# Storing a one-row decode result from two pairs of neighbouring partitions, on two queues

## The chip, the core and the metric

The kernel runs on one core of one Trainium2 chip. Its inputs lie in the chip's memory (HBM), and its result goes back there. The metric is the device time of one execution in microseconds (us). The kernel before takes 99.54 us (median of three runs, 99.52 to 99.94).

A core has five engines with instruction streams of their own: TensorE (PE, matrix products), VectorE (DVE), ScalarE (ACT), GpSimd (POOL) and SyncE (SP), which here only waits and starts transfers. They signal each other with semaphores. Transfers between HBM and the on-chip memory (SBUF, 128 partitions) are carried out by DMA engines, which SP and ACT feed through a queue each. PE writes its products to PSUM, an accumulator memory that also has 128 partitions.

## The reference

One token, a vector `x` of 1024 numbers, passes through attention over a window of 4096 cached positions and, in parallel, through a small MLP:

```python
xn = layernorm(x)
# A: 32 query heads on 4 key/value heads, the last W = 4096 positions
q = xn @ wq                                     # 1024 -> 32 x 128
p = softmax((q . k) * 128**-0.5)                # per head, over 4096 positions
A = (p . v) @ wo                                # 4096 -> 1024
# B: second layernorm, then an MLP of 3584 hidden units
B = gelu(layernorm(xn) @ w1 + b1) @ w2 + b2     # 1024 -> 3584 -> 1024
return x + A + B                                # 1 x 1 x 1024, bfloat16
```

Everything is bfloat16 in memory. The weights and the cached keys and values come to 39.86 MB, and all of it has to be read once; the result is 2 KB.

## The kernel before, in words

**Loads.** SP issues the large loads in the order w1, k, wq, then (once buffers come free) w2, v and, last, wo. Each has a semaphore of its own, or one for each chunk. wo is loaded in four chunks of 20, 8, 3 and 1 rows (`WO_CHUNKS`), where a "row" means the 1024 output columns that belong to one of 32 contraction steps of 128. ACT issues three small loads at the start, on lines 204 to 206: b1 (16 pieces of 448 bytes), x and b2 (one piece of 2048 bytes each).

**Vector times matrix.** In all products with a weight matrix the vector is the stationary operand (it is loaded into PE as weights, LDWEIGHTS) and the matrix streams through (MATMUL). PE's array is used as four column tiles of 32 columns. For w2 and wo the 1024 output columns are cut into four quarters, and quarter `a` is made in column tile `a`, so it lands in PSUM on the partitions 32a to 32a+31 of one bank (`quad`). All 28 steps of w2 and all 32 steps of wo accumulate onto the same four quarters, and before them `x` and `b2` are added there with a product with a one (line 488). One step is a call of `row`: four weight loads and four matmuls with 256 streamed columns, one for each quarter.

A weight tile has 32 columns, but only one of them is wanted. `put` is given 32 neighbouring columns of `VEC`, beginning with the wanted one, so the wanted result stands on the first partition of each quarter: 0, 32, 64 and 96. The other 31 partitions collect sums that nobody reads. `VEC` holds the MLP's hidden vector (`GT`, 28 columns), 32 zero columns, the attention's output (`OT`, 32 columns) and 32 more zero columns.

**Loops on PE.** The steps of w2 and wo are rolled into loops (`rolled`, line 160): 7 trips of 4 steps each, where one trip has 16 weight loads and 16 matmuls. The addresses are in registers. At the start of a trip every operand's address is worked out with one register addition from that of the first operand of its kind (lines 177 to 179): 15 additions for the 16 matrix operands and 3 for the 4 vector operands. Several such additions are put into one instruction, FUSED_REGOPS. After the matmuls come a further FUSED_REGOPS (line 182) and the branch back (line 184).

**The end.** The trips of the wo loop wait for a count (`s_go`) that SP raises when a chunk has landed (lines 560 to 562): the first chunk releases five trips, the second chunk two. The last four steps are written out behind the loop: steps 28 to 30 wait for the third chunk, step 31 for the fourth. The weights of step 31 are loaded early, by four matmuls with a single column (`oneb`) into a bank that nobody reads, so that only its four matmuls are left when the last chunk arrives. Then ACT copies the PSUM bank to `ORow` in SBUF (128 partitions, 256 columns each), ACT starts the store of the four wanted rows, 512 bytes each, and SP waits for it:

```python
act.wait_ge(PE.sem, C["fin"])
C["a_out"] = ACT.mark(act.activation(out=ORow[:, :], in_=PS[:, 7 * 512:7 * 512 + 256], func=ACTF.Copy))
act.wait_ge(ACT.sem, C["a_out"])
act.dma_start(out_rows, ORow[0:128:32, :]).then_inc(s_out, 16)
sp.wait_ge(s_out, 16)
```

SP has nothing to do between its last release of the wo loop and this wait.

Of the kernel before, what the change touches and what calls it, by code (L numbers as in the profile page):

```python
# [10 lines left out]
D = 1024  # L11
# [7 lines left out]
FC = F // 128  # L19
# [4 lines left out]
LOOPED = 28  # L24
STEP = 4
# [3 lines left out]
NB = 64  # L29
OUTSIDE = -1e30  # L30
PAD = 32


class Track:
# [16 lines left out]
def bass_parallel_sum__sliding_block_cached__mixer_channel_mlp__decode_kernel(  # L51
# [18 lines left out]
    pe, dve, act, pool, sp = nc.tensor, nc.vector, nc.scalar, nc.gpsimd, nc.sync  # L70

    def sems(name, n):
        return [nc.alloc_semaphore(f"{name}{i}") for i in range(n)]

    s_xrow, s_b1, s_b2, s_w1, s_w2, s_out, s_go, s_row = (
        nc.alloc_semaphore(n) for n in ("s_xrow", "s_b1", "s_b2", "s_w1", "s_w2", "s_out", "s_go", "s_row"))
# [7 lines left out]
    ACT = Track(nc, "S_ACT")  # L84
    POOL = Track(nc, "S_POOL")

    def sb(name, shape, d):
        return nc.alloc_sbuf_tensor(name, shape, d)

    f32, bf16 = dt.float32, dt.bfloat16  # L90
    identb = sb("identb", [128, 128], bf16)
# [10 lines left out]
    oneb = sb("oneb", [128, 32], bf16)  # L102
    XBR = sb("XBR", [1, 2 * D], bf16)
    XT16 = sb("XT16", [128, 16], f32)
    msx = sb("msx", [128, 8], f32)
    XNTb = sb("XNTb", [128, KC + PAD], bf16)
    YT16 = sb("YT16", [128, 16], f32)
    msy = sb("msy", [128, 8], f32)
    EXPW = sb("EXPW", [128, 1], f32)
    YTb = sb("YTb", [128, KC + PAD], bf16)  # L110
    Hs = sb("Hs", [128, 1024], bf16)
    Qs = sb("Qs", [128, 1024], bf16)
    ORow = sb("ORow", [128, 256], bf16)
# [1 line left out]
    LB = sb("LB", [128, 8 * 144], bf16)  # L115
    HT = sb("HT", [128, FC], f32)
    U2 = sb("U2", [128, FC], f32)
    VEC = sb("VEC", [128, FC + PAD + 32 + PAD], bf16)
    GT = VEC[:, 0:FC]
    OT = VEC[:, FC + PAD:FC + PAD + 32]  # L120
    MXP = sb("MXP", [128, 3], f32)
    MXH = sb("MXH", [1, HQ], f32)
    MXQ = sb("MXQ", [1, 4 * HQ], f32)
# [14 lines left out]
    W2 = W1[:, 0:FC * D]  # L138
    WA = WW[:, KC * F:KC * F + KC * NQ]
    PS = nc.alloc_psum_tensor("PS", [128, 8 * 512], f32)  # L140
# [9 lines left out]
    out_rows = out.rearrange("b s (a n) -> (b s a) n", a=4)  # L150

    C = {}
# [60 lines left out]
    def fill(out, pattern, base, step, op=ALU.not_equal, value=1.0):  # L213
        pool.wait_ge(POOL.sem, POOL.cnt)
        return POOL.mark(pool.affine_select(
            out=out, in_=out, pattern=pattern, compare_op=op, fill=value, base=base, channel_multiplier=step))

    C["oneb"] = POOL.mark(pool.memset(oneb[:, :], 1.0))
    C["onesf"] = POOL.mark(pool.memset(onesf[:, :], INV_D))
    POOL.mark(pool.memset(XNTb[:, KC:KC + PAD], 0.0))  # L220
    C["pads"] = POOL.mark(pool.memset(YTb[:, KC:KC + PAD], 0.0))

# [18 lines left out]
    C["mask"] = fill(OUTM[:, :].rearrange("k (s g) -> k s g", g=2), [[0, 256], [1, 2]], 0, -1, value=0.0)  # L241
    C["vec"] = POOL.mark(pool.memset(VEC[:, :], 0.0))
    POOL.mark(pool.memset(BLI[:, :], 1.0))
# [44 lines left out]
    for r in range(KC):  # L288
        last = pe.matmul(xt[:, r:r + 1], lhsT=XBR[0:1, r:D:KC], rhs=oneb[0:1, 0:1])  # L289
# [40 lines left out]
    def lowered(ap, weights):  # L330
        return pe.lower_ap(ap, for_matmul_weights=weights) if isinstance(ap, bass.AP) else ap

    def tile(out, lhsT, rhs, size, at, load=True, start=False):
        return pe.add_instruction(mybir.InstMatmult(  # L334
            name=nc.get_next_instruction_name(), engine=pe.engine,
            ins=[lowered(rhs, False), lowered(lhsT, True)], outs=[pe.lower_ap(out)],
            start_tensor_calc=start, stop_tensor_calc=True, bass_skip_group_check=True, ldweights=load,
            tile_size=size, tile_position=at))

    def put(out, lhsT, rhs, a, load=True, start=False):  # L340
        return tile(out, lhsT, rhs, (128, 32), (0, 32 * a), load, start)

    def full(out, lhsT, rhs, load, start=False):
        return tile(out, lhsT, rhs, (128, 128), (0, 0), load, start)

    def part(t, bank):
        at = (bank + t // 4) * 512
        return PS[32 * (t % 4):32 * (t % 4) + 32, at:at + 512]
# [3 lines left out]
    for t in range(7):  # L352
        last = tile(part(t, 0), oneb[64:65, :], b1v[:, :, :, 4 * t:4 * t + 4], (32, 32), (64, 32 * (t % 4)), t < 4, True)
# [36 lines left out]
    for i in range(8):  # L390
        n = 128 if i < 4 else 96
        last = pe.matmul(PSb[:, 2 * 1024 + 128 * i: 2 * 1024 + 128 * i + n], lhsT=Hs[0:n, 512 * (i // 4) + i % 4:512 * (i // 4 + 1):4],
                         rhs=identb[0:n, 0:n], is_transpose=True)
# [18 lines left out]
    dve.wait_ge(POOL.sem, C["consts"])  # L412
    C["d_GT"] = DVE.mark(dve.tensor_tensor(out=GT, in0=HT[:, :], in1=U2[:, :], op=ALU.mult))

# [15 lines left out]
    for i in range(8):  # L430
        last = pe.matmul(PSb[:, 7 * 1024 + 128 * i: 7 * 1024 + 128 * (i + 1)], lhsT=Qs[:, i * 128:(i + 1) * 128],
                         rhs=identb[:, :], is_transpose=True)
# [7 lines left out]
    for e in range(4):  # L440
        last = pe.matmul(PS[:, 6 * 512 + 32 * e:6 * 512 + 32 * e + 32], lhsT=REP4[:, e * 128:(e + 1) * 128], rhs=QT[:, :])
    C["rep"] = PE.mark(last)
    LB8 = LB[:, :].rearrange("p (e x) -> p e x", x=144)
    for eng, track, qs in ((dve, DVE, (0, 1)), (act, ACT, (2, 3))):
        eng.wait_ge(PE.sem, C["rep"])
        eng.wait_ge(POOL.sem, C["lb"])
        for q in qs:
            dst = LB8[32 * q:32 * q + 32, :, 32 * q:32 * q + 16]
            src = PS[32 * q:32 * q + 32, 6 * 512:6 * 512 + 128].rearrange("p (e h) -> p e h", e=8)
# [2 lines left out]

    quad = [PS[32 * a:32 * a + 32, 7 * 512:7 * 512 + 256] for a in range(4)]

    def row(vec, ws, load=True):
        for a in range(4):
            last = put(quad[a], vec, ws[a], a, load)
        return last

    def steps(label, data, c0, n, sem=None, ready=None):  # L460
        def rows(ws, vs):
            for r in range(STEP):
                row(vs[r], ws[4 * r:4 * r + 4])

        rolled(label, n // STEP, (
            (lambda o: [data[:, bass.ds(o + j * 256, 256)] for j in range(4 * STEP)], STEP * D, False),
            (lambda o: [VEC[:, bass.ds(o + c0 + r, 32)] for r in range(STEP)], STEP, True)), rows, sem, ready)

    pe.wait_ge(DVE.sem, C["lb", 1])
    pe.wait_ge(ACT.sem, C["lb", 3])  # L470
    for half in range(2):
        for i in range(NPAIR):
            for e in range(4):
                for n in range(2 * half, 2 * half + 2):
                    at = (i * 4 + n) * 2048 + e * 512
                    last = full(PS[:, n * 512:(n + 1) * 512], LB[:, e * 288 + i * 128:e * 288 + i * 128 + 128],
                                KD[:, at:at + 512], n % 2 == 0)
# [7 lines left out]
    for a in range(4):  # L485
        for i in range(2):
            src = XBR[0:1, i * D + a * 256:i * D + (a + 1) * 256]
            tile(quad[a], identb[0:1, 0:32], src, (32, 32), (0, 32 * a), i == 0, i == 0)

    for half in range(2):  # L490
        pe.wait_ge(DVE.sem, C["mx", half])
# [20 lines left out]
            in_=Pb[:, n * 512:(n + 1) * 512].rearrange("p (c i h) -> p c i h", i=NPAIR, h=16)))  # L512
    C["tot"] = DVE.mark(dve.tensor_reduce(out=SUMP[:, :], in_=SUMS[:, :], axis=AX.X, op=ALU.add))
    pe.wait_ge(s_w2, 16)
    steps("w2", W2, 0, FC)
    pe.wait_ge(DVE.sem, C["tot"])
    C["rows"] = PE.mark(pe.matmul(PS[:, 5 * 512:5 * 512 + 1], lhsT=SAME[:, :], rhs=SUMP[:, :]))
    pe.wait_ge(DVE.sem, C["zo"])
# [30 lines left out]
    for dq in range(4):  # L549
        last = pe.matmul(PS[:, 6 * 512 + 160:6 * 512 + 192], lhsT=E4[:, dq * 128:(dq + 1) * 128],  # L550
                         rhs=OD[:, dq * 32:(dq + 1) * 32], start=(dq == 0), stop=(dq == 3))
    C["o2"] = PE.mark(last)
    for _ in range(3):
        turn_over()
    dve.wait_ge(PE.sem, C["o2"])
    dve.wait_ge(DVE.sem, DVE.cnt)
    C["OT"] = DVE.mark(dve.tensor_scalar(
        out=OT, in0=PS[:, 6 * 512 + 160:6 * 512 + 192], scalar1=REC[:, 0:1], scalar2=None, op0=ALU.mult))
    went = 0
    for j, n in enumerate(WO_CHUNKS[:-2]):  # L560
        went += n
        sp.wait_ge(s_wo[j], 16)
        sp.nop(hint="wo").then_inc(s_go, went // STEP - (went - n) // STEP)
    steps("wo", WA, FC + PAD, LOOPED, s_go, C["OT"])
    pe.wait_ge(s_wo[-2], 16)
    for c in range(LOOPED, 32):
        vec = VEC[:, FC + PAD + c:FC + PAD + c + 32]
        if c == 31:
            for a in range(4):
                put(PS[32 * a:32 * a + 32, 3 * 512:3 * 512 + 1], vec, oneb[:, 0:1], a, True, True)  # L570
            pe.wait_ge(s_wo[-1], 16)
        last = row(vec, [WA[:, c * D + a * 256:c * D + (a + 1) * 256] for a in range(4)], c < 31)
    C["fin"] = PE.mark(last)

    pe.br_lt(zero, 0, on_true="L_main", on_false="L_end").branch_hint(ending)
# [1 line left out]

    act.wait_ge(PE.sem, C["fin"])
    C["a_out"] = ACT.mark(act.activation(out=ORow[:, :], in_=PS[:, 7 * 512:7 * 512 + 256], func=ACTF.Copy))  # L579
    act.wait_ge(ACT.sem, C["a_out"])  # L580
    act.dma_start(out_rows, ORow[0:128:32, :]).then_inc(s_out, 16)
    sp.wait_ge(s_out, 16)

    return nc

# [27 lines left out]
```

## Time and profile before

| what | value |
|---|---|
| median of three runs | 99.54 us (99.52 to 99.94) |
| the profiled execution's own time | 99.53 us |
| its span, first to last instruction | 98.3 us (98.28) |
| time outside the span | 1.25 us |
| read from HBM | 39.86 MB, 406 GB/s over the span |
| PE busy / DVE busy / ACT busy | 49.0 / 31.5 / 9.6 us |
| mean granted TensorE clock | 0.844 of full |
| ACT's issue of the result's store (line 581) | 603 ns, from 96.58 us on |

The profile gives times in us from the start of the span. "PE" is matmuls and "PEld" weight loads; a "q" behind an engine's name (ACTq, SPq, PEldq) means its sequencer, that is waits, branches, register arithmetic and the issuing of transfers, which do not count as busy time. The bracket at the end of a row gives the engine's idle time before it and what ended it; "issue" is idle time for which the profile shows no wait. The trace also has each transfer's packets and the moments at which a transfer's semaphore counts up. A semaphore of a transfer rises by 16 in all.

### The profile page before, as it was taken

How to read it: one execution, taken by the hardware profiler on the slowest of the kernel's cores; microseconds unless marked ns; L12 is line 12 of the kernel's file. 1: busy time of each engine (PE TensorE's matmuls, PEld its weight loads, DVE VectorE, ACT ScalarE, POOL GpSimd, SP SyncE). 2: the span in 40 equal slices, each digit the busy share in tenths (PEclk: the TensorE clock that was granted, in tenths of full speed). 3: DMA queues.
4: the chain of work that ended last, by engine and by line, in shares of the span. 5: the costliest groups of instructions: out<-in, count | busy, mean ns of one | idle time of the engine just before them, and what ended most of it. 6: DMA issues, size and time to landing. Idle time of an engine off the chain costs nothing.

```text
span 98.3 us, 1233 instructions
## 1 busy us (share of the span) xinstructions
PE 49.0 (50%) x500; PEld 18.4 (19%) x415; DVE 31.5 (32%) x42; ACT 9.6 (10%) x23; POOL 10.1 (10%) x34
## 2 busy tenths in 40 slices
PE   0000022659520700670077589993675599786671
PEld 0000022213110000100010321221433243524240
DVE  0000003270799999993002300415550001300000
ACT  0500000240400000000002200001920001000001
POOL 2000001499940000000000000000000000000000
PEclk9999999999997555559755555999999958999999
DMA  9898888999999999999988889949999979799960
GB/s 350 350 423 373 374 373 374 447 433 427 433 513 440 427 440 440 427 427 427 587 373 373 373 373 513 607 173 427 427 433 513 467 333 533 317 417 427 387 267 1
DMA packets 1773, 39.86 MB, mean 406 GB/s; under 512 B 231, under 2 KB 235, under 8 KB 493
## 3 DMA queue, kind: packets, MB, share of 16 engines
q1 hardware_dynamic: 1728, 39.85, 95.1%
q10 hardware_dynamic: 44, 0.01, 0.1%
q14 instruction: 1, 0.00, 0.0%
HBM read 39.86 MB, written 0.00 MB: 406 GB/s over the span
## 4 chain that ended last, share of the span: by engine, by line
DMA 89%; PE 4%; SPq 4%; issue 1%; ACT 0%
DMA WW<-in_A_wq_dram 47%; DMA WW<-in_A_wo_dram 42%; PE PS L334 4%; SPq L191 2%; SPq L199 1%; ACT ORow L579 0%; SPq L208 0%; SPq L370 0%
## 5 line engine op out<-in xcount | busy, mean ns | idle before, releaser
L326 DVE STREAM_TRANSPOSE KV<-KV 128x2048 bf16<-128x2048 bf16 x8 | 18.5, 2310 | 3.4 <-DMA KV<-in_A_k_cache_dram 3.2
L334 PE MATMUL PS<-WW,XNTb 128*32 x64 | 7.2, 629 | 11.9 <-SPq L370 11.9
L334 PE MATMUL PS<-WW,VEC 128*32 (+1 forms) x240 | 9.5, 275 | 4.9 <-issue 3.2
L334 PE MATMUL PS<-KV,LB 128*128 128x512 bf16 x31 | 9.0, 463 | 1.1 <-DVE LB L450 1.1
L289 PE MATMUL PS<-oneb,XBR 1*128 1x1 bf16 x8 | 0.6, 196 | 13.9 <-DMA XBR<-in_A_x_dram 13.9
L334 PEld LDWEIGHTS PS<-WW,VEC 128*32 (+1 forms) x236 | 5.1, 96 | 9.3 <-issue 9.0
L334 PE MATMUL PS<-KV 128*64 x32 | 5.3, 507 | 1.9 <-DMA KV<-in_A_v_cache_dram 1.9
L334 PE MATMUL PS<-WW,YTb 128*32 x56 | 5.1, 494 | 1.5 <-DMA WW<-in_B_w_dram 1.5
L480 DVE TENSOR_REDUCE MXP<-PS 128x1 f32<-128x1024 f32 x2 | 2.4, 1224 | 8.3 <-PE PS L334 8.3
L292 DVE COPY XT<-PS 128x8 f32<-128x8 f32 x1 | 0.2, 168 | 14.6 <-PE PS L289 14.6
L334 PEld LDWEIGHTS PS<-WW,XNTb 128*32 x32 | 1.2, 114 | 18.4 <-issue 18.4
L541 DVE SCALAR_TENSOR_TENSOR OD<-PS,BLK,OD 128x128 f32<-128x128 f32 x3 | 1.1, 351 | 10.6 <-ACT OD L538 10.5
L334 PE MATMUL PS<-OUTM,PAR 2*128 2x512 bf16 x4 | 1.9, 614 | 4.7 <-DVE HT L397 4.7
L534 PE MATMUL PS<-E,identf 128*128 128x512 f32 x8 | 3.9, 616 | 0.0
L427 DVE CAST Qs<-PS 128x512 bf16<-128x512 f32 x1 | 0.7, 691 | 8.4 <-PE PS L334 8.4
L334 PEld LDWEIGHTS PS<-KV,LB 128*128 128x128 bf16 x16 | 1.9, 117 | 7.7 <-issue 6.9
L510 DVE STREAM_TRANSPOSE KV<-KV 128x512 bf16<-128x512 bf16 x4 | 2.7, 712 | 1.8 <-ACT KV L506 1.8
L334 PEld LDWEIGHTS PS<-KV 128*64 x32 | 2.4, 142 | 4.5 <-issue 4.0
L289 PEld LDWEIGHTS PS<-oneb,XBR 1*128 1x128 bf16 x8 | 0.6, 165 | 13.9 <-issue 13.9
L506 ACT ACTIVATE KV<-PS,BIAS 128x512 bf16<-128x512 f32 x4 | 2.7, 685 | 0.0
L425 ACT ACTIVATE Qs<-PS 128x512 bf16<-128x512 f32 x1 | 0.6, 597 | 20.4 <-PE PS L334 20.4
L334 PEld LDWEIGHTS PS<-WW,YTb 128*32 x32 | 1.5, 107 | 5.4 <-issue 5.2
(93 smaller groups left out, 37.6 us busy)
## 6 DMA issues: line engine op xcount, KB each, us to landing
WW<-in_B_w_dram SPq DMA_DIRECT2D x2, 7168.0 KB, 29.9
WW<-in_A_wq_dram SPq DMA_DIRECT2D x2, 4096.0 KB, 41.7
WW<-in_A_wo_dram SPq DMA_DIRECT2D x1, 5120.0 KB, 35.0
KV<-in_A_k_cache_dram SPq DMA_DIRECT2D x2, 2048.0 KB, 26.0
KV<-in_A_v_cache_dram SPq DMA_DIRECT2D x2, 2048.0 KB, 47.1
WW<-in_A_wo_dram SPq DMA_DIRECT2D x1, 2048.0 KB, 39.5
WW<-in_A_wo_dram SPq DMA_DIRECT2D x1, 768.0 KB, 40.9
WW<-in_A_wo_dram SPq DMA_DIRECT2D x1, 256.0 KB, 41.1
```

What stands on the lines that cost most here:

```text
L191: sp.dma_start(dst[:, c0 * width:(c0 + n) * width].rearrange("p (c n) -> p c n", c=n), src[:, c0:c0 + n, :],).then_inc(semaphores[j], 16)
L199: sp.dma_start(dst[:, 2 * i * W:2 * (i + 1) * W], cache[0, 2 * i:2 * i + 2, SK - W:SK, :].rearrange("g (m b) d -> m g (b d)", m=64),).then ...
L289: last = pe.matmul(xt[:, r:r + 1], lhsT=XBR[0:1, r:D:KC], rhs=oneb[0:1, 0:1])
L326: C["kd"] = DVE.mark(dve.transpose(out=KD4[:, n], in_=KR[:, n * 2048:(n + 1) * 2048].rearrange("p (b e s) -> p b e s", b=16, e=4)))
L334: return pe.add_instruction(mybir.InstMatmult(name=nc.get_next_instruction_name(), engine=pe.engine, ins=[lowered(rhs, False), lowered(lhs ...
L425: C["a_qs"] = ACT.mark(act.activation(out=Qs[:, 0:512], in_=PS[:, 6 * 512:7 * 512], func=ACTF.Copy))
L427: C["d_qs"] = DVE.mark(dve.tensor_copy(Qs[:, 512:1024], PS[:, 7 * 512:8 * 512]))
L480: C["mx", half] = DVE.mark(dve.tensor_reduce(out=MXP[:, half:half + 1], in_=PS[:, half * 1024:(half + 1) * 1024], axis=AX.X, op=ALU.max))
L506: C["exp"] = ACT.mark(act.activation(out=Pb[:, n * 512:(n + 1) * 512], in_=PS[:, n * 512:(n + 1) * 512], func=ACTF.Exp, bias=BIAS[:, :], s ...
L510: C["tr", n] = DVE.mark(dve.transpose(out=PT.rearrange("p (i c h) -> p c i h", i=NPAIR, h=16)[:, 16 * n:16 * n + 16], in_=Pb[:, n * 512:(n ...
L534: pe.matmul(PS[:, 3 * 512:4 * 512], lhsT=identf[:, :], rhs=E4[:, 0:512])
L541: C["d_od"] = DVE.mark(dve.scalar_tensor_tensor(out=OD[:, :], in0=PS[:, 4 * 512 + 128 * c:4 * 512 + 128 * c + 128], scalar=BLK[:, c:c + 1] ...
```

## The change

The change has four parts.

1. `VEC` gets 32 zero columns in front, so that a weight tile can also *end* with the wanted column. `O0` is the new place of `OT`.
2. `row` uses two weight tiles by turns. The quarters 0 and 2 take the 32 columns that end with the wanted one, and the quarters 1 and 3 those that begin with it, as before. The result then stands on the partitions 31 and 32 and on 95 and 96: two pairs of neighbours. In the loops there are now 8 vector operands in a trip instead of 4, so 7 additions for them instead of 3; the numbers of weight loads and matmuls are the same.
3. The product that puts `x` and `b2` into the quarters uses 32 ones instead of a one and 31 zeros, so that it reaches all 32 partitions.
4. The store becomes two: ACT stores the partitions 31 and 32, SP the partitions 95 and 96. Both wait for ACT's copy, and SP then waits for both.

```diff
-    VEC = sb("VEC", [128, FC + PAD + 32 + PAD], bf16)
-    GT = VEC[:, 0:FC]
-    OT = VEC[:, FC + PAD:FC + PAD + 32]
+    VEC = sb("VEC", [128, PAD + FC + PAD + 32 + PAD], bf16)
+    GT = VEC[:, PAD:PAD + FC]
+    OT = VEC[:, O0:O0 + 32]
...
-    def row(vec, ws, load=True):
+    def row(vecs, ws, load=True):
         for a in range(4):
-            last = put(quad[a], vec, ws[a], a, load)
+            last = put(quad[a], vecs[a % 2], ws[a], a, load)
         return last
+
+    def either(o):
+        return [VEC[:, bass.ds(o - 31, 32)], VEC[:, bass.ds(o, 32)]]
...
             for r in range(STEP):
-                row(vs[r], ws[4 * r:4 * r + 4])
+                row(vs[2 * r:2 * r + 2], ws[4 * r:4 * r + 4])
...
-            (lambda o: [VEC[:, bass.ds(o + c0 + r, 32)] for r in range(STEP)], STEP, True)), rows, sem, ready)
+            (lambda o: [v for r in range(STEP) for v in either(o + c0 + r)], STEP, True)), rows, sem, ready)
...
-            tile(quad[a], identb[0:1, 0:32], src, (32, 32), (0, 32 * a), i == 0, i == 0)
+            tile(quad[a], oneb[0:1, :], src, (32, 32), (0, 32 * a), i == 0, i == 0)
...
     for c in range(LOOPED, 32):
-        vec = VEC[:, FC + PAD + c:FC + PAD + c + 32]
+        vecs = [VEC[:, O0 + c - 31:O0 + c + 1], VEC[:, O0 + c:O0 + c + 32]]
...
-    act.wait_ge(ACT.sem, C["a_out"])
-    act.dma_start(out_rows, ORow[0:128:32, :]).then_inc(s_out, 16)
-    sp.wait_ge(s_out, 16)
+    for g, eng in enumerate((act, sp)):
+        eng.wait_ge(ACT.sem, C["a_out"])
+        eng.dma_start(out_rows[2 * g:2 * g + 2, :], ORow[31 + 64 * g:33 + 64 * g, :]).then_inc(s_out, 16)
+    sp.wait_ge(s_out, 32)
```

More of the change, by code (lines that the diff above doesn't have):

```diff
@@ L31 @@
 PAD = 32
+O0 = PAD + FC + PAD
 class Track:
@@ L514, in bass_parallel_sum__sliding_block_cached__mixer_channel_mlp__decode_kernel @@
     pe.wait_ge(s_w2, 16)
-    steps("w2", W2, 0, FC)
+    steps("w2", W2, PAD, FC)
     pe.wait_ge(DVE.sem, C["tot"])
@@ L563, in bass_parallel_sum__sliding_block_cached__mixer_channel_mlp__decode_kernel @@
         sp.nop(hint="wo").then_inc(s_go, went // STEP - (went - n) // STEP)
-    steps("wo", WA, FC + PAD, LOOPED, s_go, C["OT"])
+    steps("wo", WA, O0, LOOPED, s_go, C["OT"])
     pe.wait_ge(s_wo[-2], 16)
     for c in range(LOOPED, 32):
-        vec = VEC[:, FC + PAD + c:FC + PAD + c + 32]
+        vecs = [VEC[:, O0 + c - 31:O0 + c + 1], VEC[:, O0 + c:O0 + c + 32]]
         if c == 31:
             for a in range(4):
-                put(PS[32 * a:32 * a + 32, 3 * 512:3 * 512 + 1], vec, oneb[:, 0:1], a, True, True)
+                put(PS[32 * a:32 * a + 32, 3 * 512:3 * 512 + 1], vecs[a % 2], oneb[:, 0:1], a, True, True)
             pe.wait_ge(s_wo[-1], 16)
-        last = row(vec, [WA[:, c * D + a * 256:c * D + (a + 1) * 256] for a in range(4)], c < 31)
+        last = row(vecs, [WA[:, c * D + a * 256:c * D + (a + 1) * 256] for a in range(4)], c < 31)
     C["fin"] = PE.mark(last)
```

## The prediction

> **What bounds the kernel now.** I read the chain that ended last first, then the timeline of the last microseconds, then the single lines that the change touches. The end of the chain, in the columns start, duration, what:
>
> ```profile
> 54.73 41.08 DMA WW<-in_A_wo_dram
> 95.81 0.04 issue
> 95.85 0.29 PE PS L334 x4
> 96.15 0.02 issue
> 96.17 0.38 ACT ORow L579
> ```
>
> The loads run without a gap until the last chunk of wo lands at 95.81. What comes behind it is bare: four matmuls, ACT's copy, and from 96.55 to 98.28 the store, in which no engine computes. So a gain can come only from the 1.73 us of the store, and a loss from anything that lets PE or the store be later. The timeline says how close PE stands behind the loads:
>
> ```profile
> 88.84 0.62 PE L334 MATMUL PS<-WW,VEC 128*32 x16 [0.86 <-SPq L562]
> 89.70 0.62 PE L334 MATMUL PS<-WW,VEC 128*32 x16 [0.24 <-issue]
> 90.60 0.62 PE L334 MATMUL PS<-WW,VEC 128*32 x16 [0.28 <-issue]
> 91.46 0.62 PE L334 MATMUL PS<-WW,VEC 128*32 x16 [0.24 <-issue]
> 92.33 0.62 PE L334 MATMUL PS<-WW,VEC 128*32 x16 [0.25 <-issue]
> 93.74 0.62 PE L334 MATMUL PS<-WW,VEC 128*32 x16 [0.79 <-SPq L562]
> 94.61 1.11 PE L334 MATMUL PS<-WW,VEC 128*32 x28 [0.25 <-issue]
> 95.55 0.18 PE L334 MATMUL PS<-oneb,VEC 128*32 128x1 bf16 x4
> 95.85 0.27 PE L334 MATMUL PS<-WW,VEC 128*32 128x256 bf16 x4
> ...
> 96.58 0.60 ACTq L581 DMA_DIRECT2D out_dram<-ORow  x1
> ```
>
> Trips of the wo loop follow each other by 0.87 us, of which matmuls fill 0.62; the rest is "issue", the sequencer working out addresses. Trip 6 waits 0.79 us for data. The views of single lines (count, then shortest/median/longest in ns):
>
> ```profile
> L179 PEldq FUSED_REGOPS  x70: 42/74/79, 20.7 to 94.5; - x70
> L581 ACTq DMA_DIRECT2D out_dram<-ORow x1: 603/603/603, 96.6 to 96.6; - x1
> L204 ACTq DMA_DIRECT2D KV<-in_B_b_dram x1: 632/632/632, 0.8 to 0.8; - x1
> L205 ACTq DMA_DIRECT2D XBR<-in_A_x_dram x1: 887/887/887, 1.5 to 1.5; - x1
> L206 ACTq DMA_DIRECT2D XBR<-in_B_b_dram x1: 213/213/213, 2.4 to 2.4; - x1
> L208 SPq DMA_DIRECT2D WW<-in_B_w_dram x1: 375/375/375, 0.8 to 0.8; - x1
> L191 SPq DMA_DIRECT2D WW<-in_A_wo_dram x4: 333/428/433, 53.4 to 54.7; - x4
> ```
>
> **The change, part by part. The wider VEC, the ones, the alternating tiles.** The counts of weight loads (x16 a trip) and matmuls stay; POOL's clearing of VEC (0.19 us at 23.48) grows from 124 to 156 columns, POOL ends its last work at 28.3, and VEC is first read at 69. Cost nothing; if that cover went, a clearing of 32 columns by itself is 0.12 us (line 218).
>
> **The address additions.** A trip has 15 + 3 = 18 additions now and 15 + 7 = 22 after. The 70 records on L179 are 8 + 8 (the h and q loops with 6 additions, 1 record a trip), 7 x 3 for w2, 4 x 3 for p·v (14 additions) and 7 x 3 for wo: six additions fit into one. So 22 need 4 records instead of 3. In the trace the three of trip 6 start at 93.342, 93.474 and 93.607, and the first weight load at 93.731: 0.133 us each, although one is only 0.074 long. No matmul runs meanwhile, so a trip becomes 0.87 + 0.13 = 1.00 us.
>
> In w2 that is 7 x 0.133 = 0.93 us. It is hidden: the loop's last matmuls end at 75.00, the product of line 517 behind them at 75.31, and then PE waits until 77.21, 1.90 us, for the v cache that lands at 76.23. After the change line 517 ends at 76.24; p·v starts as before. If that cover were gone, the next one is 0.86 us of idle time ahead of 88.84.
>
> In wo it nearly uses up the slack. Trip 1 is released by data at 88.43 as before. Trip 5 left the sequencer free at 92.79; five longer trips make it 92.79 + 0.66 = 93.45, so trip 6 no longer waits for the second chunk (93.34) but begins 0.11 late. Trip 7 begins at 94.46 instead of 94.22, and its first matmuls at 94.61 + 0.24 + 0.13 = 94.99. Four matmuls take 0.11 (16 of them start over 0.44), so trip 7 goes on to 95.43, steps 28 to 30 to 95.76 (they waited for the third chunk until 95.21 before, not any more), and the early weight load of step 31, at 95.55 before, comes at 95.76 and is done by some 95.78. The last chunk lands at 95.81. So 0.03 to 0.07 us are left and the last matmuls stay at 95.85: cost 0. Bounds: 0, and about +0.1 should trips stretch a little more (the p·v loop's third record, with only 2 additions, still takes 0.12, so a fourth can't be much cheaper or dearer).
>
> **The store.** Before: issue at 96.58 for 0.60; by the trace's packet records the four pieces of 512 bytes start between 97.82 and 97.88; their counts arrive at 98.187, 98.201, 98.214 and 98.246. That is 0.64 from the issue's end to the first piece and 0.37 to its count. After: ACT's own two pieces. Does ACT's issue get shorter? L204 has 16 pieces and took 632 ns, L581 has 4 and took 603: 2.4 ns a piece, so two pieces fewer are worth 0.005. I take 0.60. Its bounds are the other two of ACT's issues, each of one piece: 213 (a gain of 0.39) and 887 (a loss of 0.28). I stay at 603 because L206 came straight behind two others, while L204 and L581 each are the first after a pause. The last of four counts came 0.059 behind the first; with two it should be 0.014 to 0.02: a gain of 0.04.
>
> SP's half: SP sits at its wait, ACT's signal took 0.03 to reach ACT's own sequencer and takes about 0.03 to SP (the release of line 562 was seen 0.03 us after the landing). SP's first issues after a pause took 333 (L191) and 375 ns (L208), and the first load's packets came 1.00 us after its issue's start. So SP's pieces should start near 97.6, 0.2 ahead of ACT's, and be hidden behind them. Bound: SP's longest issue, 665 ns in the view of line 199, would end it 0.06 after ACT's. Behind the waiting SP nothing is queued but its last wait; SP's queue has been empty since 95.81.
>
> The Trainium skill's page "DMA: Bandwidth & Descriptors" (section "Issuing engines are not separate DMA queues", and "Why a DMA increments its semaphore by 16 and not by 1" on how many engines) says that transfers of both queues run on the same DMA engines, and that a transfer of two rows takes the two lowest-numbered. By it the two halves share two engines where four were used, and the gain of the skew is partly lost: with a piece of 27 to 33 ns from the packet records, the sum would be 99.52 instead of 99.49. No run here shows it yet.
>
> **The sum**, against the profiled execution's 99.53 (span 98.28 and 1.25 around it; 0.01 under the median): PE 0, ACT's copy 0, ACT's issue 0, skew -0.04, SP hidden 0: 99.49, so 99.5. Both pieces of unknown cost, at their ends: -0.39 - 0.04 gives 99.10; +0.28 + 0.1 gives 99.91.
>
> **The rivals.** *PE becomes late at half the clock (slower).* The trace grants half the clock from 78.40 to 81.81, after a stretch in which PE was busy for 44%, and the full clock after stretches of 59 to 72%:
>
> ```profile
> 64.74:68.16 3.42, 2.02 (x16) 0.44 (x8) 1.64 (x2) 0.13 (x1) 0.00 (x0) 1.00 0.82 350
> 74.98:78.40 3.42, 1.52 (x18) 0.94 (x16) 0.00 (x0) 0.00 (x0) 0.00 (x0) 1.00 1.02 438
> 78.40:81.81 3.41, 3.41 (x20) 1.55 (x18) 0.00 (x0) 0.00 (x0) 0.00 (x0) 0.50 1.23 529
> 88.64:92.05 3.41, 2.46 (x64) 1.38 (x64) 0.00 (x0) 0.00 (x0) 0.00 (x0) 1.00 1.03 437
> ```
>
> (Columns: stretch, length, busy time of PE, PEld, DVE, ACT, POOL, then the granted clock.) Longer trips lower PE's share in wo from 0.62/0.87 = 71% to 0.62/1.00 = 62%, just above the lowest that kept the clock. Should it fall at 95, each of nine groups of four matmuls behind 94.99 takes 0.11 more: +1.0 less the 0.07 of slack, about 100.4. It decides as soon as PE is ready after 95.81. Against it: 2.12 of 3.41 (62%) in the stretch from 92.05 kept the clock.
>
> The skill's page "TensorE: Matmul & The Clock Gate" (section "Why this matters for your kernels") lets the rate fall only after a window of idling, gaps over about 3 us. By that rule this rival has no room and the time is 99.49. The trace differs, with its fall after 44%.
>
> *The two issues hinder each other.* At the start both sequencers issue at once, and L205 took 887 ns where the same form took 213 later. If ACT's store pays that: 99.49 + 0.28 = 99.8. It decides once the cost of issuing side by side exceeds 0.04. Against it: L204 and L208, truly started together, took 632 and 375, about what they take alone.
>
> *ACT's issue really shrinks with the neighbouring rows.* If it falls to the 213 of L206: 99.1. For it: no row of the trace shows a store of two neighbouring partitions; against it: L204 with 16 pieces.
>
> **How the numbers follow.** Forecast 0.58 (99.35 to 99.65); issues hindering each other 0.12 (99.8); PE late 0.20 (100.1 to 100.5); shorter issue 0.10 (99.0 to 99.1). A measurement here can tell 0.5% from no change, 0.50 us, so 99.04 and 100.04 are the bounds. PE late is slower, and the issues' rival passes the bound in a third of its cases: 0.25. The shorter issue passes it in most of its chance's better half: 0.08. The rest, 0.67, is within. Leaving out the worst of PE late and the best of the shorter issue, 99.1 to 100.3 holds 8 in 10.
>
> **What would show it.** Right: 4 records of line 179 in each w2 and wo trip, trips 1.00 us apart, trip 6 without its wait on line 562, the last four matmuls at 95.85, ACT's issue near 0.6 and SP's near 0.35, the span 98.2. Wrong: the last matmuls not waiting for the last chunk; a clock of 0.50 behind 92; either issue above 0.65, or SP's counts arriving after ACT's.

## The result and the profile after

The changed kernel takes 99.13 us (median of six executions, 99.07 to 99.15) against 99.55 for the kernel before: a ratio of 0.9955 with a 95% interval of 0.9942 to 0.9968. That is 0.42 us less. The forecast was 99.5. The time lies inside its range of 99.1 to 100.3 and inside "within 0.5%", but at the lower edge of both, and where the time comes from is not what the forecast's sum said.

The profiled execution took 99.14 us with a span of 97.88, so 1.25 us lie around the span, as before. All of the gain is in the span. The timeline of the wo loop and of the end in the kernel after (start, duration, engine, line, operation; in the bracket the idle time before it and what ended it):

```profile
88.95 0.62 PE L335 MATMUL PS<-WW,VEC 128*32 x16 [1.10 <-SPq L566]
89.97 0.62 PE L335 MATMUL PS<-WW,VEC 128*32 x16 [0.39 <-issue]
90.94 0.62 PE L335 MATMUL PS<-WW,VEC 128*32 x16 [0.35 <-issue]
...
93.90 0.62 PE L335 MATMUL PS<-WW,VEC 128*32 x16 [0.35 <-issue]
...
94.92 0.95 PE L335 MATMUL PS<-WW,VEC 128*32 x28 [0.40 <-issue]
...
95.69 0.18 PE L335 MATMUL PS<-oneb,VEC 128*32 128x1 bf16 x4
95.81 0.27 PE L335 MATMUL PS<-WW,VEC 128*32 128x256 bf16 x4
96.13 0.38 ACT L583 ACTIVATE ORow<-PS 128x256 bf16<-128x256 f32 x1 [13.30 <-PE PS L335]
96.54 0.33 SPq L586 DMA_DIRECT2D out_dram<-ORow  x1
96.54 0.27 ACTq L586 DMA_DIRECT2D out_dram<-ORow  x1
```

Trips are 1.00 us apart now, the sixth trip (93.90) no longer waits for data but for "issue", and the early weight load of step 31 has moved from 95.55 to 95.69. The last four matmuls still begin 0.04 us behind the landing of the last chunk (95.77 here, 95.81 before). So PE kept up. (The profile's chain of this run leads back through the trips and not to the chunk, because it has PE busy with the single-column matmuls right up to the last four. What shows that the data held them is the 0.04 us: it is 0.04 in the traces of all runs below too, though their last chunks land anywhere between 95.68 and 96.05, except in the one run whose trips are longer still.) The gain is in the last two rows: ACT's issue takes 0.27 us instead of 0.60. The view of the two lines concerned:

```profile
L180 PEldq FUSED_REGOPS  x84: 42/74/79, 20.7 to 94.8; - x84
L586 SPq DMA_DIRECT2D out_dram<-ORow x1: 330/330/330, 96.5 to 96.5; - x1
L586 ACTq DMA_DIRECT2D out_dram<-ORow x1: 265/265/265, 96.5 to 96.5; - x1
```

There are 84 address records, 14 more than before: one in each of the 2 x 7 trips.

What comes after the issue is told by the records of packets and of the counts of the store's semaphore in the two traces. All are in us, and the last column is the whole end: from the start of the last four matmuls to the last count.

| kernel | ACT's copy ends | issue starts (ACT / SP) | first piece (ACT / SP) | last count (ACT / SP) | last matmuls to last count |
|---|---|---|---|---|---|
| before | 96.55 | 96.58 / none | 97.82 / none | 98.25 / none | 2.39 |
| after | 96.51 | 96.54 / 96.54 | 97.30 / 97.33 | 97.67 / 97.85 | 2.04 |

From an issue's start to the first piece took 1.24 us before and takes 0.76 (ACT) and 0.79 (SP) now. This saves 0.48. From the first piece to the last count took 0.43 before and takes 0.37 for ACT's pair, but 0.52 for SP's, although SP's pieces start only 0.03 behind ACT's. (Both halves raise the same semaphore. Its four counts come in two close pairs, 97.65 and 97.67, then 97.83 and 97.85, and I take the earlier pair for ACT's.) So SP's half, which the forecast had hidden behind ACT's, is the one that ends last. The span is shorter by 0.39: 0.35 in this end, and 0.04 because the last chunk landed that much earlier.

### The profile page after: what moved, and what is told of

It is laid out like the page before. It is cut to its first block, busy times and chain, and to the rows that moved or that the text cites. A ratio compares the mean times of both kernels' runs of the same rounds, so it can differ in the third digit from the quotient of the medians.

```text
span 97.9 us, 1248 instructions
## 1 busy us (share of the span) xinstructions
PE 49.4 (50%) x500; PEld 18.7 (19%) x415; DVE 31.5 (32%) x42; ACT 9.6 (10%) x23; POOL 10.2 (10%) x34
## 4 chain that ended last, share of the span: by engine, by line
DMA 83%; PE 9%; issue 3%; SPq 2%; ACT 0%
DMA WW<-in_A_wq_dram 47%; DMA WW<-in_A_wo_dram 36%; PE PS L335 9%; SPq L200 1%; SPq L192 1%; SPq L209 0%; ACT ORow L583 0%; SPq L371 0%; SPq L566 0%
## 5 line engine op out<-in xcount | busy, mean ns | idle before, releaser
L335 PE MATMUL PS<-WW,VEC 128*32 (+1 forms) x240 | 10.5, 308 | 4.7 <-issue 3.5
L335 PE MATMUL PS<-KV,LB 128*128 128x512 bf16 x31 | 8.5, 445 | 1.0 <-DVE LB L451 1.0
L335 PEld LDWEIGHTS PS<-WW,VEC 128*32 (+1 forms) x236 | 5.6, 105 | 9.8 <-issue 9.3
L335 PE MATMUL PS<-WW,YTb 128*32 x56 | 6.1, 564 | 1.5 <-DMA WW<-in_B_w_dram 1.5
```

Source lines behind the costliest of these rows:

```text
L335: return pe.add_instruction(mybir.InstMatmult(name=nc.get_next_instruction_name(), engine=pe.engine, ins=[lowered(rhs, False), lowered(lhs ...
```

## The experiments

Two theories could explain the short issue: the number of pieces (two in place of four), or the distance of their partitions (1 in place of 32). The first four runs separate these, and look at SP's late counts. In all of them and in those below I quote the ratio to the kernel before in the same series, and the end from the last four matmuls to the last count in the profiled execution (2.39 before, 2.04 after).

**One store of four distant partitions, issued by SP.**

```diff
-    act.wait_ge(ACT.sem, C["a_out"])
-    act.dma_start(out_rows, ORow[0:128:32, :]).then_inc(s_out, 16)
+    sp.wait_ge(ACT.sem, C["a_out"])
+    sp.dma_start(out_rows, ORow[0:128:32, :]).then_inc(s_out, 16)
```

> The kernel before, with its one store of the partitions 0, 32, 64 and 96 issued by SP instead of ACT. If the long issue (603 ns) belongs to the four pieces or to their distance, SP's issue is long too, near 0.6 us, and the time stays at 99.5. If it belongs to ACT, SP's issue takes 0.33 us as in its other first issues, and since the four pieces go to four DMA engines, whose counts came within 0.06 us of each other, the last count arrives near 97.7 and the time is 99.0, below the changed kernel's 99.13.

Measured: 99.63 us, ratio 1.0001 (0.9993 to 1.0010), end 2.40. The issue on SP:

```profile
L581 SPq DMA_DIRECT2D out_dram<-ORow x1: 656/656/656, 96.8 to 96.8; - x1
```

The long issue does not belong to ACT. SP needs 0.66 for the same transfer, and its first piece comes 1.25 us after the issue's start.

**The store split in two, partitions as before.**

```diff
-    act.dma_start(out_rows, ORow[0:128:32, :]).then_inc(s_out, 16)
-    sp.wait_ge(s_out, 16)
+    for g, eng in enumerate((act, sp)):
+        eng.wait_ge(ACT.sem, C["a_out"])
+        eng.dma_start(out_rows[2 * g:2 * g + 2, :], ORow[64 * g:64 * g + 64:32, :]).then_inc(s_out, 16)
+    sp.wait_ge(s_out, 32)
```

> The kernel before, with its store split in two and nothing else: ACT stores the partitions 0 and 32, SP 64 and 96. If the issue got short because there are two pieces instead of four, ACT's issue takes 0.27 us here as well and the time is 99.1, that of the changed kernel. If it got short because the partitions are neighbours, ACT's issue stays near 0.6 us and the time is 99.45 to 99.55.

Measured: 99.70 us, ratio 1.0019 (1.0009 to 1.0029), end 2.60. The two issues:

```profile
L582 SPq DMA_DIRECT2D out_dram<-ORow x1: 633/633/633, 96.5 to 96.5; - x1
L582 ACTq DMA_DIRECT2D out_dram<-ORow x1: 585/585/585, 96.5 to 96.5; - x1
```

Two pieces that are 32 partitions apart take as long to issue as four. The number of pieces is out as a cause, and the split by itself makes the kernel a little slower (0.14 us in the median): ACT's first piece comes 1.23 us after its issue's start, SP's only after 1.50, 0.27 behind. SP's store of four such pieces, issued alone in the run before, needed 1.25. So of two stores of this kind that are issued together, one starts its pieces some 0.25 us late, although the issues themselves take no longer.

**Four neighbours, one store by ACT.**

```diff
-    act.dma_start(out_rows, ORow[0:128:32, :]).then_inc(s_out, 16)
+    act.dma_start(out_rows, ORow[0:4, :]).then_inc(s_out, 16)
```

> The kernel before, with one store of four pieces from ACT as before, but from the partitions 0 to 3, which are neighbours (three of them hold sums that are not wanted, so the output is not the result). By the theory of the number of pieces ACT's issue stays at 0.6 us and the time at 99.5. By the theory of the neighbours it falls to about 0.27 us and the time to 99.1 or less.

Measured: 99.07 us, ratio 0.9950 (0.9937 to 0.9964), end 1.91.

```profile
L581 ACTq DMA_DIRECT2D out_dram<-ORow x1: 281/281/281, 96.6 to 96.6; - x1
```

With the split left out and only the partitions moved together, the whole gain is there, and a little more. First piece 0.76 us after the issue's start, as in the changed kernel. So it is how the partitions lie: a step of 32 from one to the next, or of 1. That distant partitions belong to different quarters of 32 is not the reason, since 31 and 32 in the changed kernel do so too.

**Both pairs stored by ACT.**

```diff
-    for g, eng in enumerate((act, sp)):
+    for g, eng in enumerate((act, act)):
```

> The changed kernel, with both pairs stored by ACT, one after the other. In the changed kernel SP's counts came 0.18 us behind ACT's, although its packets started only 0.03 later. If this is because both halves go through the same two DMA engines, the second pair's counts here too come at least 0.18 behind the first's, and the time is 99.13 or, as the second issue starts 0.3 us later, up to 99.4. If SP's queue itself is the slow one, both pairs' counts follow their packets by 0.33 us, and the second pair ends about 0.3 behind the first, 99.2 to 99.3 in all.

Measured: median 99.27 us, ratio 0.9993 (0.9967 to 1.0018), end 2.16. The 12 executions reach from 99.08 to 100.21, which is taken up below. The second issue starts 0.31 us behind the first, its pieces 0.30 behind, and the counts of both pairs come 0.37 behind their first pieces. So two pairs whose pieces are 0.3 us apart do not delay each other. Nor is it enough that two queues are in use: in the split run both were, with pieces 0.27 apart, and both halves' last counts came 0.38 behind their first pieces. This leaves two readings of SP's late counts, which the next run separates: they come from pieces that start at nearly the same time, or from SP's queue.

**SP's pair alone.**

```diff
-    for g, eng in enumerate((act, sp)):
-        eng.wait_ge(ACT.sem, C["a_out"])
-        eng.dma_start(out_rows[2 * g:2 * g + 2, :], ORow[31 + 64 * g:33 + 64 * g, :]).then_inc(s_out, 16)
-    sp.wait_ge(s_out, 32)
+    sp.wait_ge(ACT.sem, C["a_out"])
+    sp.dma_start(out_rows[2:4, :], ORow[95:97, :]).then_inc(s_out, 16)
+    sp.wait_ge(s_out, 16)
```

> The changed kernel with ACT's store left out: only SP stores its pair, so half the result is missing. In the changed kernel SP's counts came 0.50 us behind its packets, ACT's 0.35, and the two kernels in which the halves' packets were 0.3 apart had 0.37 for both. If the halves hinder each other at the DMA engines that they share, SP's counts come 0.35 to 0.38 behind its packets here and the time is about 98.98. If SP's queue is slower by nature, they come 0.50 behind and the time stays at 99.13.

Measured: 99.21 us, ratio 0.9951 (0.9934 to 0.9968), end 1.86. The issue takes the same 330 ns as beside ACT's, and the last count comes 0.37 us behind the first piece. Together with the run before, this shows that the later half's counts are delayed by 0.15 us when the halves' pieces start within 0.03 us: the end is 1.86 for one pair and 2.04 for two. The median does not show it so clearly. It lies above the expected 98.98, in a series in which the kernel before had 99.81.

**The tiles and the longer trips alone, with the old store.**

```diff
-    for g, eng in enumerate((act, sp)):
-        eng.wait_ge(ACT.sem, C["a_out"])
-        eng.dma_start(out_rows[2 * g:2 * g + 2, :], ORow[31 + 64 * g:33 + 64 * g, :]).then_inc(s_out, 16)
-    sp.wait_ge(s_out, 32)
+    act.wait_ge(ACT.sem, C["a_out"])
+    act.dma_start(out_rows, ORow[0:128:32, :]).then_inc(s_out, 16)
+    sp.wait_ge(s_out, 16)
```

> The changed kernel's tiles and loops with the store of the kernel before (one, by ACT, of the partitions 0, 32, 64 and 96; two of these rows are then not the wanted ones, so the output is not the result). If the longer trips are hidden, as the prediction has it, ACT's issue is back at 0.60 us, the last four matmuls still begin 0.04 us behind the last chunk, and the time is 99.5 to 99.6. If the longer trips do cost something that the quicker store concealed, the time is above 99.65. A theory from the run before: two more instructions on PE make its program long enough that 16 KB of code are fetched near the end (a packet at 96.8), and now and then the program's end waits for them; then some executions take 100 us and more with an unchanged span.

Measured: 99.70 us, ratio 1.0001 (0.9981 to 1.0022), end 2.39, and the issue is back at its old length. The last rows of its timeline:

```profile
95.68 0.18 PE L335 MATMUL PS<-oneb,VEC 128*32 128x1 bf16 x4
95.85 0.27 PE L335 MATMUL PS<-WW,VEC 128*32 128x256 bf16 x4
96.17 0.38 ACT L583 ACTIVATE ORow<-PS 128x256 bf16<-128x256 f32 x1 [14.91 <-PE PS L335]
96.59 0.60 ACTq L585 DMA_DIRECT2D out_dram<-ORow  x1
```

The median is above the 99.65 that would have spoken against hidden trips, but the kernel before had 99.81 in this series, and the ratio is 1. The 14 added address records cost nothing in the span. The last matmuls begin at 95.85, as in the kernel before.

**One more instruction in each trip.**

```diff
         pe.br(f"L_{label}")
         nc.switch_bb(f"L_{label}", parent=None)
         if sem is not None:
             pe.wait_ge(sem, trip)
+        if label == "wo":
+            pe.wait_ge(DVE.sem, 1)
```

> The changed kernel with one more instruction in each of the seven trips of the wo loop, a wait for a count that was reached long before. Such a wait takes 0.11 us of the sequencer in the trace of before, so the trips are 1.11 us apart and PE is 0.74 us later at the end of the loop. If the longer trips of the change used up the slack but for 0.03 to 0.1 us, the last four matmuls come 0.64 to 0.71 us later than the last chunk allows, and the time is 99.75 to 99.85. If there is much more slack than that, the time stays nearer to 99.1.

Measured: 99.80 us, ratio 1.0029 (1.0006 to 1.0053). Ten of the 12 executions have spans of 98.3 to 98.7, mostly 98.5 where the changed kernel in the same series has 97.8 to 98.0. That is 0.6 to 0.65 for 0.74 us of added sequencer time, so about 0.1 us of slack was left in the changed kernel's wo loop. The other two have spans of 99.2 and 99.3, and the profiled one is of these:

```profile
88.88 0.62 PE L337 MATMUL PS<-WW,VEC 128*32 x16 [1.01 <-SPq L568]
89.99 0.62 PE L337 MATMUL PS<-WW,VEC 128*32 x16 [0.48 <-issue]
91.11 0.78 PE L337 MATMUL PS<-WW,VEC 128*32 x16 [0.50 <-issue]
92.19 5.00 PE L337 MATMUL PS<-WW,VEC 128*32 x76 [0.30 <-issue]
96.97 0.23 PE L337 MATMUL PS<-oneb,VEC 128*32 128x1 bf16 x4
97.05 0.38 PE L337 MATMUL PS<-WW,VEC 128*32 128x256 bf16 x4
```

Its stretches (length, busy time of PE, PEld, DVE, ACT, POOL, granted clock, DMA):

```profile
84.60:88.00 3.40, 3.27 (x12) 1.49 (x11) 0.25 (x1) 0.00 (x0) 0.00 (x0) 1.00 0.80 342
88.00:91.40 3.40, 1.53 (x44) 0.99 (x48) 0.00 (x0) 0.00 (x0) 0.00 (x0) 1.00 1.00 424
91.40:94.80 3.40, 2.95 (x54) 1.30 (x48) 0.00 (x0) 0.00 (x0) 0.00 (x0) 0.51 0.94 387
```

In the stretch from 88.00 to 91.40 PE was busy for 1.53 of 3.40 us (45%). Then the clock fell to half and stayed there to the end. The matmuls ran without a pause and still came late: the last four began 1.33 us behind the landing of the last chunk (95.72). Of this, some 0.6 belongs to the longer trips, as in the ten other executions, and the rest, some 0.7 (99.2 against 98.5 in the span), to the clock. This is the prediction's first rival as it would look.

The changed kernel is not safe from such a fall. In its first profile the clock is full from 80.4 to 97.5. In the profile of its repetition (the last experiment below) it is at half from 89.45 to 92.87, in the midst of the wo loop:

```profile
89.45:92.87 3.42, 3.11 (x56) 1.39 (x48) 0.00 (x0) 0.00 (x0) 0.00 (x0) 0.50 0.94 397
```

```profile
89.01 0.67 PE L335 MATMUL PS<-WW,VEC 128*32 x16 [2.70 <-SPq L566]
89.99 3.57 PE L335 MATMUL PS<-WW,VEC 128*32 x64 [0.31 <-issue]
93.96 0.62 PE L335 MATMUL PS<-WW,VEC 128*32 x16 [0.40 <-issue]
...
95.88 0.27 PE L335 MATMUL PS<-WW,VEC 128*32 128x256 bf16 x4
```

It cost nothing there. The trips still follow each other by 0.96 to 1.02 us, as in the first profile: the 16 matmuls of a trip start over 0.63 us instead of 0.35, and that still fits into a trip. The clock was full again for the last two trips, and the last four matmuls began 0.04 us behind the last chunk (95.84).

**The neighbours without the longer trips.** The vectors stand twice in VEC, 31 columns apart, so that a single tile has the wanted column first and last. The last four steps, which are written out, use the two tiles of the changed kernel. The core of the edit, on the kernel before (the store is the changed kernel's):

```diff
+APART = 31
+O0 = 2 * PAD + APART
...
-    OT = VEC[:, FC + PAD:FC + PAD + 32]
+    GT2 = VEC[:, APART:APART + FC]
+    OT = VEC[:, O0:O0 + APART]
+    OT2 = VEC[:, O0 + APART:O0 + APART + 32]
...
-    C["d_GT"] = DVE.mark(dve.tensor_tensor(out=GT, in0=HT[:, :], in1=U2[:, :], op=ALU.mult))
+    for g in (GT, GT2):
+        C["d_GT"] = DVE.mark(dve.tensor_tensor(out=g, in0=HT[:, :], in1=U2[:, :], op=ALU.mult))
...
-    steps("wo", WA, FC + PAD, LOOPED, s_go, C["OT"])
+    steps("wo", WA, O0, LOOPED, s_go, C["OT"])
```

> The two pairs of neighbours without the longer trips: the vectors stand twice in VEC, 31 columns apart, so that one weight tile both begins and ends with the wanted column. The loops are those of the kernel before (18 additions, 3 records a trip), VectorE has two small writes more, the store is that of the changed kernel. If the longer trips cost nothing, the time is that of the changed kernel, 99.1, with trips of 0.87 us. If they cost something, it is less by that. PE's program has the length of the one before, so by the theory of the fetched code no packet of 16 KB comes near the end and no execution takes 100 us.

Measured: 99.25 us (median of five executions, in a series in which the kernel before had 99.81), ratio 0.9945 (0.9932 to 0.9959), end 2.05. Its timeline has the old trips back, and the sixth waits for data again:

```profile
91.61 0.62 PE L338 MATMUL PS<-WW,VEC 128*32 x16 [0.28 <-issue]
92.47 0.62 PE L338 MATMUL PS<-WW,VEC 128*32 x16 [0.23 <-issue]
93.84 0.62 PE L338 MATMUL PS<-WW,VEC 128*32 x16 [0.75 <-SPq L569]
```

The ratio is that of the changed kernel's first executions within the intervals. Undoing the longer trips gains nothing in the median, which is the other half of the evidence that they were hidden.

**One store of two neighbours.** To be rid of the second store, VectorE copies the upper half of the partitions onto the lower half, beside ACT's copy:

```diff
-    C["a_out"] = ACT.mark(act.activation(out=ORow[:, :], in_=PS[:, 7 * 512:7 * 512 + 256], func=ACTF.Copy))
+    C["a_out"] = ACT.mark(act.activation(out=ORow[0:64, 0:256], in_=PS[0:64, 7 * 512:7 * 512 + 256], func=ACTF.Copy))
+    dve.wait_ge(PE.sem, C["fin"])
+    C["d_out"] = DVE.mark(dve.tensor_copy(ORow[0:64, 256:512], PS[64:128, 7 * 512:7 * 512 + 256]))
+    act.wait_ge(DVE.sem, C["d_out"])
...
+    act.dma_start(out_rows.rearrange("(h p) n -> p h n", p=2),
+                  ORow[31:33, :].rearrange("p (h n) -> p h n", h=2)).then_inc(s_out, 16)
```

> The changed kernel with another end: ACT copies the partitions 0 to 63 and VectorE 64 to 127, the latter onto the partitions 0 to 63 beside them, so that all four quarters stand on the two neighbouring partitions 31 and 32, and ACT stores them with one transfer. If the distance of the partitions is what costs and the collision of two stores the rest, the issue takes 0.27 to 0.33 us, the last count comes 0.37 to 0.45 us behind the first piece, and the time is 98.9 to 99.05. If VectorE's copy or its signal is slower than ACT's by more than 0.15 us, or a transfer with two pieces a partition costs as much as one of distant partitions, there is no gain over 99.13.

Measured: median 99.23 us, ratio 0.9977 (0.9947 to 1.0007), end 1.95. The profile shows what was expected:

```profile
96.17 0.38 ACT L583 ACTIVATE Qs<-PS 64x256 bf16<-64x256 f32 x1 [14.91 <-PE PS L335]
96.17 0.43 DVE L585 CAST Qs<-PS 64x256 bf16<-64x256 f32 x1 [12.25 <-PE PS L335]
96.64 0.28 ACTq L588 DMA_DIRECT2D out_dram<-Qs  x1
```

The last count comes 0.40 behind the first piece, and the end is 0.09 us shorter than in the changed kernel. The median, above the expected 98.9 to 99.05, does not show it: four of the 12 executions took 99.8 to 100.5, and the kernel before had 99.81 in this series.

**Both together**: the vectors twice, and the one store.

> Both findings together: the vectors stand twice, 31 columns apart, so the loops are those of the kernel before, and the four quarters are copied onto two neighbouring partitions by ACT and VectorE and stored with one transfer by ACT. By the times of the parts (the last count 1.19 us behind the last of the copies, where the changed kernel has 1.34, and a second copy that ends 0.05 later) the median is 0.10 us below the changed kernel's, 0.994 of the kernel before. PE's program is as short as before, so no execution takes 0.6 us more with the usual span.

Measured: 99.18 us (98.96 to 99.49), ratio 0.9961 (0.9946 to 0.9976), end 1.95. The changed kernel in the same series had 99.28. This is the version to keep. Its median is 0.10 below the changed kernel's, as expected, its slowest execution 0.73 below, but the ratio falls short of the expected 0.994; that the median is lower is within the scatter of the executions, while the profile's 0.09 in the end appears in both kernels with that store.

**The changed kernel once more, and the kernel before made longer.** In the changed kernel's first profile, the list of queues has one line that the kernel before does not have:

```profile
q8 instruction: 1, 0.02, 0.1%
```

It is a fetch of 16 KB of instructions at 96.83. The kernel with both pairs on ACT has one at 96.74. In that kernel and others with the alternating tiles some executions took about 1 us more, with the usual span. So the changed kernel was run 12 times more, and the kernel before with PE's program made longer by two instructions, as many as the change adds to it (one more address instruction in each of two loops):

```diff
+    for n in (1, 2, 3):
+        pe.wait_ge(DVE.sem, n)
     pe.wait_ge(s_w2, 16)
     steps("w2", W2, 0, FC)
```

(Three waits are written, of which two become instructions of their own.)

> The changed kernel once more, for more executions of it. By the theory of the fetched code the median is 0.995 of the kernel before, and one to three of 12 executions take over 0.6 us more with the usual span. Without it all lie within 0.2 us, as the first six did.

> The kernel before with PE's program longer by two instructions, as that of the changed kernel is: waits on counts long reached, ahead of the w2 loop, where they are hidden. In the kernels with this longer program some executions took 1 to 2 us more outside an unchanged span, and in two of their traces 16 KB of instructions are fetched at 96.7 to 96.8. If the length of PE's program does it, the median stays at that of the kernel before, but some of 12 executions take over 0.6 us more than the median with the usual span. If something else in the changed kernels does it (the tiles, the longer trips, the other store), none does.

Measured, the changed kernel: median 99.28 us, ratio 0.9979 (0.9956 to 1.0002); ten executions between 99.18 and 99.34, and two at 100.07 and 100.22 with spans of 97.8 and 97.9, so 2.3 us outside the span. The gain in the span is there again (97.85 in the median against 98.3). But the time outside the span was 1.46 us in the median, where the kernel before had 1.26 in this series, and the interval of the ratio now just includes 1. The six executions of the first result had no such long ones, and so showed the gain larger and steadier than it is. The kernel before with two more instructions: 99.61 us, ratio 1.0006 (0.9988 to 1.0023), never more than 1.6 us outside the span.

The time outside the span, over all executions here: the six kernels with alternating tiles in the loops spent 1.9 us or more in 13 of 78 executions (2.0 to 2.4 each); those with the old loops, the kernel before among them, in none of 152, where 1.6 is the most. It goes with the alternating tiles in the loops or their longer trips. The longer program by itself was not enough in 12 executions; at a rate of 13 in 78 none in 12 happens by chance about once in nine times, so the fetched code is not ruled out either. In the two traces with the fetch the time outside the span is the usual 1.25. What makes these executions long stays open.

## Why the prediction was right or wrong

**The wider VEC, the ones, the counts of instructions:** right. Weight loads and matmuls are 415 and 500 in both profiles.

**The address additions:** right, closely. Four records a trip (84 in all), trips 1.00 apart, trip 6 without its wait, and the last four matmuls held by the data. The early weight load came at 95.69 where the sum said 95.76. The slack left was put at 0.03 to 0.07 and measured as about 0.1.

**ACT's issue:** wrong, and this is the step that failed. It was taken as 0.60 with the argument that 16 pieces took 632 ns and four took 603, "2.4 ns a piece, so two pieces fewer are worth 0.005". The number of pieces is indeed worth nothing (two distant pieces: 585 and 633), but the argument asked only about the number, while the change also altered the distance. The issue took 265, close to the bound of 213 that the sum set aside because it came "straight behind two others". That had no part in it here: with both pairs on ACT the first issue took 265 and the second, straight behind it, 267. The third rival, the shorter issue with neighbouring rows, was given a chance of 0.10 and 99.1 us, and it is what happened: 99.13. That this agrees to 0.03 us is chance, since two things that this rival did not count came in as well and nearly cancelled. One is that the lie of the partitions is felt not only in the issue. The wait from the issue's end to the first piece fell as well, from 0.64 to 0.49, so issue and wait together, 0.00 in the sum, measured -0.48. The other is SP's half, below.

**The skew:** right for ACT's pair. Its first piece to its last count went from 0.43 to 0.37, -0.06 where -0.04 was forecast.

**SP hidden behind ACT:** wrong in its outcome. SP's issue was close (330, where 333 to 375 was taken). But its pieces came with ACT's, since ACT's were earlier by more than SP's were (97.30 for 97.82, 97.33 for some 97.6), and of two pairs so close the later one is delayed: SP's last count is 0.18 behind ACT's. This term was 0.00 and measured +0.18. The Trainium skill's page "DMA: Bandwidth & Descriptors" (sections "Issuing engines are not separate DMA queues" and "Why a DMA increments its semaphore by 16 and not by 1") had spoken of this: by it, both halves run on the same two DMA engines. The direction agrees with the trace; the price, put at 0.03 from the length of a piece, is 0.15 in the runs (0.52 beside ACT's pair, 0.37 alone). The page states the sharing; that it is the reason for the delay is not shown, since no record here names the engines that carry the pieces.

**The first rival, PE late at half the clock:** it did not happen. PE was in time in both profiled executions of the changed kernel, in one of them although the clock fell to half in the wo loop. The run with one more instruction a trip shows what the rival would look like, and bears out its price: by the trace's records, groups of four matmuls start 0.21 us apart there at half the clock, and 0.11 apart at the full one in the changed kernel. The prediction judged the risk by PE's busy share in a stretch of 3.4 us. The traces of the runs do not bear out the share as the measure: the clock fell after stretches with 58% (71.12 to 74.53 in the kernel with the vectors twice) and 57% (68.22 to 71.63 in the run with the old store), and held after one with 53% (75.62 to 79.03 in the kernel with both findings). What decides it stays open. The Trainium skill's page "TensorE: Matmul & The Clock Gate" (section "Why this matters for your kernels") gives a window of idling, a gap of over about 3 us, as what brings the clock back to half; the falls after 44% and 45% differ from that, with no gap over 1.90 and 1.01 us in the stretches before them.

**The second rival, hindering issues:** it exists for stores of distant partitions, but not as a longer issue (585 and 633 in the split run): SP's pieces started 1.50 us after its issue's start, against 1.25 alone. Between stores of neighbours little of it is seen (0.79 beside ACT's, 0.76 alone).

**The number:** luck in part. The three terms of the store measured -0.48, -0.06 and +0.18, together -0.36, where the sum had -0.04. Had SP's half been hidden, as the sum had it, the time would have been about 98.95 (an estimate, 99.13 less 0.18), below the range. One of the prediction's own signs of being wrong was seen: SP's counts arrived after ACT's. Its 0.08 for a time below 99.04 does not follow either: most of the better half of a chance of 0.10 is less than 0.05.

## What to carry to other kernels

The issue of a small store can be a fixed cost that is set by how the partitions lie, not by their number or the engine; where a store ends a kernel, it is worth choosing the layout for it ahead of splitting it. When the trace of before has no row of the new form, ask of every property that the change alters whether a row varies it; here the rows varied the number of pieces, and none the distance. Two small stores that start within 0.03 us of each other can cost more than one that does the work of both (an end of 2.04 us with two, 1.95 with one).

## What the runs showed of the hardware

Stores of 512-byte pieces from partitions that are 32 apart took 585 to 656 ns to issue on ACT and on SP alike, with two pieces or four. From neighbouring partitions they took 265 to 330 ns, with two or four pieces or with two pieces a partition. From the issue's start the first piece started after 1.23 to 1.25 us in the former case (1.50 where the other queue issued too) and after 0.75 to 0.79 us in the latter. Why distance costs this is not told by any record here, and no distance between 1 and 32 was tried. When two stores of neighbouring partitions on two queues started their pieces 0.03 us apart, the later last count came 0.52 us behind its first piece; alone, or 0.3 apart, it was 0.37.
